# Attention times values with one 64-key by 128-query matmul in place of two 64x64 ones

## The chip, the core and the metric

The kernel runs on one core of one Trainium2 chip. The metric is the device time of one execution in microseconds (us); for several runs, their median. A profiled execution also has a span, from its first to its last instruction, which is a little shorter than its device time. TensorE (PE) does the matmuls and, as instructions of their own (PEld), loads their weights; VectorE (DVE) and ScalarE (ACT) do the elementwise work; GpSimd (POOL) and SyncE (SP) issue most of the DMAs.

## The reference

Sliding-window causal attention, followed by a SwiGLU feed-forward block. There are 8 batches, 8 heads, 576 positions and 64 dimensions per head; the window is 64 keys, the position itself included.

```python
scores = scale * np.matmul(q, k.transpose(0, 1, 3, 2))
mask = (rel >= 0) & (rel < window)        # rel = query position - key position, window = 64
...
attn = attn / (np.sum(attn, axis=-1, keepdims=True) + 1e-09)
out = np.matmul(attn, v)
...
g = x @ w_gate
silu = g * (1.0 / (1.0 + np.exp(-g)))
val = x @ w_val
return (silu * val @ w_out).astype(np.float32)
```

The rows x are the 4608 positions of all batches, each with its 8 x 64 attention outputs; d_model is 512 and d_ff is 1536.

## The kernel before

The 4608 rows are cut into 36 chunks of 128 rows, and for the feed-forward part into 9 groups of 512 rows. A chunk holds two blocks of 64 queries (w = 0 and 1). A batch has 9 blocks, so a block with (2n + w) % 9 == 0 is the first of its batch and has no earlier keys; eight of the 36 chunks hold such a block, here called edge chunks.

Scores (S, matmul on L780). For each head the scores stand with keys on the partitions and queries in the free dimension, in the tile pt. Partitions 0 to 63 hold the chunk's own first 64 keys against all its 128 queries. Partitions 64 to 127 hold, for the queries of block 0, the last 64 keys of the chunk before, and, for those of block 1, the chunk's own last 64 keys. ScalarE takes the exponential into pt (L790), and VectorE multiplies by a mask (L795, function M). The ring pt has 4 buffers, so chunk n uses buffer n % 4.

Probabilities times values. Each head has up to four matmuls, one per half of the partitions (kp = 0 or 1) and query block (w). The weights are a 64x64 piece of pt, and the moving operand is 64 rows of va: the 64 value columns of a head and a column of ones for the sum. The output stands on PSUM partitions 64w to 64w + 63. So each matmul uses a quarter of the array: kp picks the rows, w the columns. For single chunks (n up to 19) this is `A_split`, with the matmul on L832; its two PSUM banks hold heads 0 to 3 and 4 to 7. It runs in two phases (step 0 and 1), so that at one time one bank takes results from rows 0 to 63 only and the other from rows 64 to 127 only: kp = half ^ step. The phases are placed by `A0` and `A1` in the opening, and by `A` afterwards, which puts the scores of the next chunk between them. From chunk 20 on, `A_pair` treats two chunks together (matmul on L905), with three banks: heads 0 to 6 of each chunk, and head 7 of both; here kp = step ^ i for chunk i of the pair, and kp = step for head 7. An edge block leaves out the matmul with the earlier keys.

After that VectorE divides by the sums (L872 to L878, and in pairs from L921 on), the rows are transposed on TensorE (X, L947) or by a DMA on SP's queue (XD, L962), and the feed-forward part follows: gate and value matmuls (FM, L977), tanh on ScalarE (L996), two products on VectorE (L1005, L1007), and the output matmul (OM, L1017).

The order of the work is written out by hand: a list `OPENING` up to about 60 us, and then loops in `build` over groups c, row blocks u and steps s, in which `block(n)` (chunks 12 to 19) and `pair(n)` (20, 22, ..., 34) are put between feed-forward steps. Each engine plays its instructions in the order of recording; a dependency graph from read and write keys adds the semaphore waits. K and Q of chunk n + 4 are transposed by DMA on SP's queue (`TD`, L748 and L751), issued at the end of `block(n)`.

At the place `alone` (L1254), one feed-forward step after `block(19)`, `build` records scores, mask and a merging of the PSUM rings. `block(19)` has already made the scores of chunk 20. The kernel before makes those of chunk 20 there once more, and never those of chunk 21: the pair (20, 21) uses for chunk 21 what chunk 17 left in that buffer of pt.

A second program, `general`, is for inputs out of the usual range; it is built into the kernel, and isn't run here.

Of the kernel before, what the change touches and what calls it, by code (L numbers as in the profile page):

```python
# [14 lines left out]
BPB = S // 64  # L15
# [495 lines left out]
class _Kernel:  # L511
# [292 lines left out]
    def A_split(self, n):  # L804
        g = self.g
        ip = n % self.NP
        va, vp, pt = self.va[n % self.NV], self.va[(n - 1) % self.NV], self.pt[ip]
        bb = [self.bank("a") for _ in range(2)]
        av = [b[:, 0:260].rearrange("p (h x) -> p h x", h=4) for b, _ in bb]
        seq = {}  # L810
        for step in range(2):
            for j in range(4):
                for half in range(2):
                    kp = half ^ step
                    for w in range(2):
                        if kp == w or (2 * n + w) % BPB:
                            seq.setdefault((half, w), []).append((step, j, kp))

        def phase(step):
            def pe(e):  # L820
                for j in range(4):
                    for w in range(2):
                        for half in range(2):
                            q = seq[half, w]
                            key = (step, j, half ^ step)
                            if key not in q:
                                continue
                            kp, h = half ^ step, 4 * half + j
                            vv = vp if kp > w else va
                            ks = slice(64 * kp, 64 * kp + 64)  # L830
                            ws = slice(64 * w, 64 * w + 64)
                            r = e.matmul(av[half][ws, j, :], pt[ks, h, ws], vv[ks, h, 0:65],  # L832
                                         start=key == q[0], stop=key == q[-1])
                return r
            return pe

        vk = [("va", m % self.NV, j) for m in ((n - 1, n) if n else (n,)) for j in range(2)]
        vk += [("va", m % self.NV) for m in ((n - 1, n) if n else (n,))]
        rd = [("pt", ip, 0), ("pt", ip, 1)] + vk
        wr = [bk for _, bk in bb]  # L840

        def run(step, *after):
            return g.op("pe", phase(step), reads=rd, writes=wr, after=list(after))

        return run, bb, av
# [35 lines left out]
    def A_pair(self, n, S0, S1):  # L881


        g = self.g
        nn = (n, n + 1)
        masks = S0()
        banks = [self.bank("a") for _ in range(3)]
        pt = [self.pt[m % self.NP] for m in nn]
        seqs, last = [[], []], {}
        for step in range(2):  # L890
            for h, i in [(h, i) for h in range(7) for i in range(2)] + [(7, 0), (7, 1)]:
                kp = step if h == 7 else step ^ i
                b, col = (2, 65 * i) if h == 7 else (i, 65 * h)
                for w in range(2):
                    if kp == w or (2 * nn[i] + w) % BPB:
                        seqs[step].append((i, h, kp, w, b, col))
                        last.setdefault((b, w), []).append((step, i, h))

        def phase(step):
            def pe(e):  # L900
                for i, h, kp, w, b, col in seqs[step]:
                    ks, ws = slice(64 * kp, 64 * kp + 64), slice(64 * w, 64 * w + 64)
                    vv = self.va[(nn[i] - 1 if kp > w else nn[i]) % self.NV]
                    q, key = last[b, w], (step, i, h)
                    r = e.matmul(banks[b][0][ws, col:col + 65], pt[i][ks, h, ws], vv[ks, h, 0:65],  # L905
                                 start=key == q[0], stop=key == q[-1])
                return r
            return pe

        rd = [("pt", m % self.NP, h) for m in nn for h in range(2)]  # L910
        rd += [("va", m % self.NV, j) for m in (n - 1,) + nn for j in range(2)] + [("va", m % self.NV) for m in (n - 1,) + nn]
        wr = [bk for _, bk in banks]
        first = g.op("pe", phase(0), reads=rd, writes=wr)
        masks = masks + S1()
        g.op("pe", phase(1), reads=rd, writes=wr, after=[first])
        xb = [self.xb[m % 4].rearrange("p (h d) -> p h d", h=H) for m in nn]
        for i, m in enumerate(nn):
            bank, bk = banks[i]
            a = bank[:, 0:455].rearrange("p (h x) -> p h x", h=7)
            rc = self.rc[:, 8 * m:8 * m + 7]  # L920
            g.op("dve", lambda e, rc=rc, a=a: e.reciprocal(rc.unsqueeze(2), a[:, :, 64:65]), reads=[bk],  # L921
                 writes=[("rc", 2 * m), ("rc", 2 * m + 1)])
            rb = rc.unsqueeze(2).to_broadcast([128, 7, 64])
            xo = xb[i][:, 0:7, :]
            g.op("dve", lambda e, xo=xo, rb=rb, a=a: e.tensor_tensor(xo, a[:, :, 0:64], rb, ALU.mult),
                 reads=[bk, ("rc", 2 * m)], writes=[("xb", m % 4, 0), ("xb", m % 4, 1)])
        bank, bk = banks[2]
        a = bank[:, 0:130].rearrange("p (i x) -> p i x", i=2)
        rc = self.rc[:, 8 * n:8 * n + 16].rearrange("p (i h) -> p i h", i=2)[:, :, 7:8]
        g.op("dve", lambda e: e.reciprocal(rc, a[:, :, 64:65]), reads=[bk],  # L930
             writes=[("rc", 2 * m + 1) for m in nn])
        for i, m in enumerate(nn):
            xo = xb[i][:, 7, :]
            r1 = self.rc[:, 8 * m + 7:8 * m + 8]
            g.op("dve", lambda e, xo=xo, r1=r1, i=i: e.tensor_scalar(xo, a[:, i, 0:64], r1, None, ALU.mult),
                 reads=[bk, ("rc", 2 * m + 1)], writes=[("xb", m % 4, 0), ("xb", m % 4, 1)])
        return masks
# [251 lines left out]
    def build(self):  # L1189
# [17 lines left out]
        def block(n):  # L1207
            if n >= NCH:
                return
            load(n + 6)  # L1210
            self.A(n, n + 1 if n + 1 < NCH else None)
            self.XD(n)
            if n + 4 < NCH:
                self.TD(n + 4)

        pair_from = 20

        def pair(n):
            ring, i = self.rot["*"]
            ring = [ring[(i + j) % 8] for j in range(8)]  # L1220
            more = n + 2 < NCH
            for m in (n + 6, n + 7):
                load(m)
            masks = self.A_pair(n, *(lambda m=m: self.S(m, True) if more else [] for m in (n + 2, n + 3)))
            if more:
                self.rot["*"] = ([ring[j] for j in (7, 0, 1, 5, 6, 2, 3, 4)], 0)
            for m in (n + 4, n + 5):
                if m < NCH:
                    self.TD(m)
            for m in (n, n + 1):  # L1230
                self.XD(m)
            for f in masks:
                f()
# [5 lines left out]
        for n in range(pair_from, NCH, 2):  # L1239
            c, r = divmod(n - 6, 4)  # L1240
# [4 lines left out]
        for c in range(2, NFC):  # L1245
            if c == 6:
                self.hint_at = len(self.g.ops)
            for u in range(4):
                late = c == NFC - 1 and u == 3
                for s in range(3):  # L1250
                    self.F(c, 3 * u + s)
                    if s != 1 and (c, u, s) in place:
                        block(place[c, u, s])
                    if (c, u, s) == alone:  # L1254
                        self.S(pair_from)
                        self.M(pair_from)
                        self.share()
                    if s == 1 and not late and c < cp:
                        self.O(c - 1, u, "f" if (c, u, s) in place else "a")
                    if s == 1 and (c, u, s) in place:  # L1260
                        block(place[c, u, s])
                    if c == NFC - 1 and (u, s) in judged:
                        self.judge(judged[u, s])
                if c >= cp and not late:
                    self.O(c - 1, u, "a", "dve" if (c, u) in pairs else "act")
                if (c, u) in pairs:
                    pair(pairs[c, u])
                if late:
                    self.general_at = len(self.g.ops)
                    self.O(c - 1, u)  # L1270
# [46 lines left out]
```

## Time and profile before

| what | value |
|---|---|
| device time, median of 3 runs | 335.17 us (333.53 to 335.91) |
| device time of the profiled execution | 333.98 us |
| span of the profiled execution | 331.4 us |
| matmuls, and as many weight loads | 3511 |
| of these probabilities times values, L832 and L905 | 600 and 488 |
| read from and written to HBM | 37.75 MB and 9.44 MB |

How to read the lines in the prediction. A group line gives the source line, engine, operation and tiles, for matmuls the shape of the weight tile (64*64 means 64 rows by 64 columns), the form of the moving operand, and the count; behind the first bar stand the busy time of the group in us and the mean of one in ns, behind the second the engine's idle time ahead of them. Matmuls are pipelined: their durations overlap, and their ends are modelled by the profiler. A timeline row gives a start, a length from the first start to the last end of a merged run, and the count; two groups that overlap appear as rows that overlap. A row of the table of windows gives the window, its length, and for each engine its busy time and instruction count, then the clock granted to TensorE.

### The profile page before, as it was taken

What the parts mean: (1) busy time and instruction counts of PE and PEld (TensorE: products, weight loads), DVE (VectorE), ACT (ScalarE), POOL (GpSimd) and SP (SyncE); (2) the same over time, 40 slices, a digit from 0 to 9 for tenths busy, and PEclk for the clock granted to TensorE, in tenths of its full rate; (3) what the DMA queues carried; (4) which work ended last, traced back from release to release, by engine and by line L of the source; (5) the groups of instructions that cost most, each with busy time, mean ns of one, the idle gap of its engine ahead of it and who ended that gap; (6) DMA issues with size and microseconds to landing.
All of it is one profiled execution on the core that took longest, in us unless ns stands there. A gap on an engine that the chain in (4) does not pass through costs nothing.

```text
span 331.4 us, 8401 instructions
## 1 busy us (share of the span) xinstructions
PE 323.7 (98%) x3511; PEld 166.2 (50%) x3511; DVE 224.7 (68%) x490; ACT 128.3 (39%) x239; POOL 110.7 (33%) x141
## 2 busy tenths in 40 slices
PE   7799899999999999999999999999999999999996
PEld 3587475555444544445454545454545444444444
DVE  5578896967866866667777777767676776565520
ACT  2756644343333543434242433333424222232222
POOL 7999993194364453333435151000000000000000
PEclk9999999999999999999999999999999999999999
DMA  9999999999999999999999999715140202000012
GB/s 169 150 177 169 171 191 141 171 135 170 169 167 148 191 154 174 173 160 158 149 126 108 135 124 130 128 53 110 47 113 33 65 33 64 34 32 35 35 60 102
DMA packets 169515, 40.19 MB, mean 121 GB/s; under 512 B 155904, under 2 KB 164992, under 8 KB 169472
## 3 DMA queue, kind: packets, MB, share of 16 engines
q0 software_dynamic: 117312, 18.36, 82.8%
q1 hardware_dynamic: 50976, 20.66, 33.3%
q10 hardware_dynamic: 1184, 0.59, 0.7%
q8 instruction: 28, 0.46, 0.6%
q14 instruction: 15, 0.12, 0.1%
HBM read 37.75 MB, written 9.44 MB: 142 GB/s over the span
## 4 chain that ended last, share of the span: by engine, by line
PE 92%; DVE 2%; POOL 2%; DMA 1%; ACT 1%; issue 1%; POOLq 0%
PE ps L977 56%; PE ps L1017 27%; PE ps L780 3%; PE ps L832 2%; PE ps L905 2%; DMA kn<-in_k_dram 1%; PE ps L1049 1%; PE ps L947 1%; DVE uu L1005 1%; POOL va L710 1%; POOL qn L647 1%; DVE hT L1007 0%; PE ps L730 0%; ACT sig L996 0%; ACT qT L664 0%
## 5 line engine op out<-in xcount | busy, mean ns | idle before, releaser
L1005 DVE SCALAR_TENSOR_TENSOR uu<-sig,ps 128x512 bf16<-128x512 bf16 (+2 forms) x122 | 76.0, 623 | 57.5 <-ACT sig L996 57.5
L977 PE MATMUL ps<-xT,Wg 128*128 128x512 bf16 (+2 forms) x488 | 113.7, 355 | 0.3
L977 PE MATMUL ps<-xT,Wv 128*128 128x512 bf16 (+2 forms) x488 | 113.3, 355 | 0.0
L996 ACT ACTIVATE sig<-ps 128x512 bf16<-128x512 f32 (+2 forms) x122 | 66.7, 551 | 82.7 <-PE ps L977 82.4
L1017 PE MATMUL ps<-Wo,hT 128*128 128x512 bf16 x420 | 95.9, 379 | 0.0
L1007 DVE SCALAR_TENSOR_TENSOR hT<-uu,ps 128x512 bf16<-128x512 bf16 (+2 forms) x122 | 76.3, 626 | 4.2
L977 PEld LDWEIGHTS ps<-xT,Wv 128*128 128x128 bf16 x488 | 47.1, 98 | 46.5 <-DVE uu L1005 0.2
L977 PEld LDWEIGHTS ps<-xT,Wg 128*128 128x128 bf16 x488 | 44.6, 98 | 42.2 <-issue 0.4
L1017 PEld LDWEIGHTS ps<-Wo,hT 128*128 128x128 bf16 x420 | 40.9, 98 | 49.2
L647 POOL DMA_DIRECT2D qn<-in_q_dram x38 | 34.9, 932 | 68.2 <-DMA qT<-qn 60.8
L790 ACT ACTIVATE pt<-ps 128x512 bf16<-128x512 f32 x72 | 38.0, 600 | 41.3 <-PE ps L780 41.2
L710 POOL DMA_DIRECT2D va<-in_v_dram x40 | 35.4, 911 | 24.0 <-PE ps L905 19.4
L664 ACT ACTIVATE ost<-ps 128x512 f32<-128x512 f32 (+2 forms) x26 | 15.0, 577 | 64.1 <-PE ps L1017 63.1
L647 POOL DMA_DIRECT2D kn<-in_k_dram x38 | 34.9, 936 | 0.9 <-issue 0.7
L795 DVE TENSOR_TENSOR pt<-pt,mask 128x512 bf16<-128x512 bf16 x64 | 23.8, 419 | 1.2 <-ACT pt L790 1.0
L666 DVE COPY ost<-ps 128x512 f32<-128x512 f32 (+1 forms) x12 | 7.9, 657 | 23.7 <-PE ps L1017 11.9
L878 DVE TENSOR_TENSOR xb<-ps,rc 128x256 bf16<-128x256 f32 x40 | 17.0, 425 | 1.4
L780 PE MATMUL ps<-qT,kT 64*64 64x64 bf16 (+1 forms) x864 | 16.0, 203 | 0.7 <-DVE kT L666 0.3
L780 PEld LDWEIGHTS ps<-qT,kT 64*64 64x64 bf16 x864 | 12.5, 108 | 6.2 <-issue 3.0
L832 PE MATMUL ps<-va,pt 64*64 64x65 bf16 x600 | 12.4, 196 | 1.5 <-issue 1.0
L832 PEld LDWEIGHTS ps<-va,pt 64*64 64x64 bf16 x600 | 8.3, 106 | 8.7 <-issue 3.0
L875 DVE RECIPROCAL rc<-ps 128x4 f32<-128x4 f32 x40 | 7.0, 175 | 6.1 <-PE ps L832 6.1
(57 smaller groups left out, 103.1 us busy)
## 6 DMA issues: line engine op xcount, KB each, us to landing
out_dram<-ost SPq DMA_DIRECT2D x35, 256.0 KB, 3.1
va<-in_v_dram POOLq DMA_DIRECT2D x32, 128.0 KB, 16.8
qn<-in_q_dram POOLq DMA_DIRECT2D x30, 128.0 KB, 15.2
kn<-in_k_dram POOLq DMA_DIRECT2D x30, 128.0 KB, 15.4
Wo<-in_moe_w_out_dram POOLq DMA_DIRECT2D x2, 768.0 KB, 16.2
Wg<-in_moe_w_gate_dram POOLq DMA_DIRECT2D x5, 256.0 KB, 6.7
Wv<-in_moe_w_val_dram POOLq DMA_DIRECT2D x5, 256.0 KB, 7.3
fk<-in_k_dram SPq DMA_DIRECT2D x1, 512.0 KB, 4.9
```

The lines of the kernel that those rows point to most:

```text
L647: self.g.op("pool", lambda e, d=d, a=a: e.dma_start(d, a), writes=ks, dma=True)
L710: g.op("pool", lambda e, d=d, a=a: e.dma_start(d, a), writes=ks, dma=True)
L780: r = e.matmul(sv[h][o:o + 64, c, q0:q1], self.kT[ps, c, kk:kk + 64], qT[ps, c, q0:q1], start=not biased, stop=not biased or c == 3 and kk ...
L790: g.op("act", lambda e, po=po, si=si: e.activation(po, si, ACTF.Exp, scale=SCALE), reads=[bk], writes=[pk])
L795: "dve", lambda e: e.tensor_tensor(po, po, m, ALU.mult), reads=[pk, "mask"], writes=[pk]))
L832: r = e.matmul(av[half][ws, j, :], pt[ks, h, ws], vv[ks, h, 0:65], start=key == q[0], stop=key == q[-1])
L878: g.op("dve", lambda e, xo=xo, rb=rb, a=av[half]: e.tensor_tensor(xo, a[:, :, 0:64], rb, ALU.mult), reads=[bk, ("rc", ir)], writes=[("xb", ...
L977: r = e.matmul(bank[:, 0:n], W[:, kk, f * 128:f * 128 + 128], xT[:, kk, t0:t1], start=(kk == 0), stop=(kk == NK - 1))
L996: self.g.op("act", lambda e: e.activation(sig[:, 0:n], G[:, 0:n], ACTF.Tanh, scale=0.5), reads=[gk], writes=[("sig", i)])
L1005: g.op("dve", lambda e: e.scalar_tensor_tensor(uu[:, 0:n], sig[:, 0:n], 1.0, G[:, 0:n], ALU.add, ALU.mult), reads=[("sig", i), gk], writes ...
L1007: g.op("dve", lambda e: e.scalar_tensor_tensor(hT[:, f, t0:t1], uu[:, 0:n], 0.5, V[:, 0:n], ALU.mult, ALU.mult), reads=[("uu", i), vk], wr ...
L1017: r = e.matmul(OB[:, :], hT[:, f, 128 * u:128 * u + 128], self.Wo[:, f, :], start=(f == 0), stop=(f == NF - 1))
```

## The change

In chunks without an edge block, the two matmuls of a head with kp = 0 become one: its weights are the 64 keys by all 128 queries, and its output is on all 128 PSUM partitions. The two with kp = 1 stay as they are, since their values come from two different chunks or blocks. A full chunk then has 24 matmuls in place of 32. In a pair with an edge chunk the head 7 of both keeps the old form. The order of the matmuls stays what it was, with the merged one at the place of its w = 0 part. At `alone` the scores and mask of chunk 21 are made in place of those of chunk 20.

```diff
@@ A_split
-        seq = {}
+        seq, last, full = [[], []], {}, all((2 * n + w) % BPB for w in range(2))
         for step in range(2):
             for j in range(4):
-                for half in range(2):
-                    kp = half ^ step
-                    for w in range(2):
+                for w in range(2):
+                    for half in range(2):
+                        kp = half ^ step
                         if kp == w or (2 * n + w) % BPB:
-                            seq.setdefault((half, w), []).append((step, j, kp))
+                            if not (full and kp == 0):
+                                seq[step].append((half, j, kp, w, w + 1))
+                            elif w == 0:
+                                seq[step].append((half, j, 0, 0, 2))
+                            last.setdefault((half, w), []).append((step, j))
...
+                for half, j, kp, w0, w1 in seq[step]:
+                    h, q = 4 * half + j, last[half, w0]
+                    vv = vp if kp > w0 else va
+                    ks, ws = slice(64 * kp, 64 * kp + 64), slice(64 * w0, 64 * w1)
+                    r = e.matmul(av[half][ws, j, :], pt[ks, h, ws], vv[ks, h, 0:65],
+                                 start=(step, j) == q[0], stop=(step, j) == q[-1])
@@ A_pair
+        full = [all((2 * m + w) % BPB for w in range(2)) for m in nn]
+        full.append(full[0] and full[1])
...
                     if kp == w or (2 * nn[i] + w) % BPB:
-                        seqs[step].append((i, h, kp, w, b, col))
+                        if not (full[b] and kp == 0):
+                            seqs[step].append((i, h, kp, w, w + 1, b, col))
+                        elif w == 0:
+                            seqs[step].append((i, h, 0, 0, 2, b, col))
                         last.setdefault((b, w), []).append((step, i, h))
...
-                    ks, ws = slice(64 * kp, 64 * kp + 64), slice(64 * w, 64 * w + 64)
+                    ks, ws = slice(64 * kp, 64 * kp + 64), slice(64 * w, 64 * w1)
@@ build
                     if (c, u, s) == alone:
-                        self.S(pair_from)
-                        self.M(pair_from)
+                        self.S(pair_from + 1)
+                        self.M(pair_from + 1)
```

More of the change, by code (lines that the diff above doesn't have):

```diff
@@ L809, in A_split @@
         av = [b[:, 0:260].rearrange("p (h x) -> p h x", h=4) for b, _ in bb]
-        seq = {}
+        seq, last, full = [[], []], {}, all((2 * n + w) % BPB for w in range(2))
         for step in range(2):
             for j in range(4):
-                for half in range(2):
-                    kp = half ^ step
-                    for w in range(2):
+                for w in range(2):
+                    for half in range(2):
+                        kp = half ^ step
                         if kp == w or (2 * n + w) % BPB:
-                            seq.setdefault((half, w), []).append((step, j, kp))
+                            if not (full and kp == 0):
[3 more added lines that the diff above has]
+                            last.setdefault((half, w), []).append((step, j))
         def phase(step):
             def pe(e):
[L821 to L833, printed above, removed]
+                for half, j, kp, w0, w1 in seq[step]:
[4 more added lines that the diff above has]
+                                 start=(step, j) == q[0], stop=(step, j) == q[-1])
                 return r
@@ L900, in pe @@
             def pe(e):
-                for i, h, kp, w, b, col in seqs[step]:
-                    ks, ws = slice(64 * kp, 64 * kp + 64), slice(64 * w, 64 * w + 64)
+                for i, h, kp, w, w1, b, col in seqs[step]:
+                    ks, ws = slice(64 * kp, 64 * kp + 64), slice(64 * w, 64 * w1)
                     vv = self.va[(nn[i] - 1 if kp > w else nn[i]) % self.NV]
```

## The prediction

> **What bounds the kernel now.** I read the page's engine table first, then its slices, then the chain of work that ended last, and then a table of windows that cuts the span into opening, middle and end.
>
> ```profile
> PE 323.7 (98%) x3511; PEld 166.2 (50%) x3511; DVE 224.7 (68%) x490; ACT 128.3 (39%) x239; POOL 110.7 (33%) x141
> ...
> PE 92%; DVE 2%; POOL 2%; DMA 1%; ACT 1%; issue 1%; POOLq 0%
> ```
>
> ```profile
> core 0: us, PE busy (x) PEld busy (x) DVE busy (x) ACT busy (x) POOL busy (x), PEclk, DMA share, GB/s
> 0.00:8.00 8.00, 6.31 (x30) 2.75 (x31) 4.59 (x21) 2.12 (x3) 6.02 (x15) 1.00 1.09 170
> 8.00:13.00 5.00, 4.39 (x150) 2.95 (x148) 2.80 (x9) 4.13 (x8) 5.00 (x8) 1.00 2.17 141
> 13.00:20.00 7.00, 5.40 (x131) 3.63 (x129) 4.10 (x16) 3.64 (x7) 7.00 (x10) 1.00 1.75 165
> 20.00:60.00 40.00, 38.81 (x515) 26.49 (x513) 33.23 (x86) 21.64 (x48) 32.33 (x40) 1.00 1.89 172
> 60.00:150.00 90.00, 90.00 (x1067) 44.46 (x1066) 64.94 (x144) 37.05 (x67) 40.49 (x48) 1.00 1.84 164
> 150.00:271.00 121.00, 120.94 (x1308) 58.30 (x1306) 86.25 (x171) 42.96 (x77) 19.89 (x24) 1.00 0.88 100
> ```
>
> TensorE is the bound: 98% busy, 92% of the chain, and from 60 to 271 us without a gap. Its clock is granted in full. So a microsecond that the changed matmuls add or save in that stretch is a microsecond of the span; no other engine covers it. Before 60 us TensorE is idle for 0.61 + 1.60 + 1.19 = 3.4 us after the start-up; at most that much of an added cost could hide there.
>
> The matmuls that change are two groups, probabilities times values for single chunks (L832) and for pairs (L905):
>
> ```profile
> L832 PE MATMUL ps<-va,pt 64*64 64x65 bf16 x600 | 12.4, 196 | 1.5 <-issue 1.0 <-ACT pt L790 0.2
> L905 PE MATMUL ps<-va,pt 64*64 64x65 bf16 x488 | 7.6, 193 | 0.1
> ...
> L947 PE MATMUL ps<-ident,xb 128*128 128x128 bf16 x40 | 3.6, 220 | 0.4 <-DVE xb L878 0.3
> ```
>
> The means (about 0.19 us) are latencies that overlap; what one costs must be read from the starts. Here is one whole visit, the attention of chunk 19, with the feed-forward matmuls (L977) on either side; each row gives the start, the time from first start to last end, and the count:
>
> ```profile
> 137.10 0.38 PE L977 MATMUL ps<-xT,Wv 128*128 128x512 bf16 x1
> 137.41 0.32 PE L832 MATMUL ps<-va,pt 64*64 64x65 bf16 x16
> 137.56 0.42 PE L780 MATMUL ps<-qT,kT 64*64 64x128 bf16 x24
> 137.81 0.32 PE L832 MATMUL ps<-va,pt 64*64 64x65 bf16 x16
> 138.06 0.39 PE L977 MATMUL ps<-xT,Wg 128*128 128x512 bf16 x1
> ```
>
> Three things are in it. First, the pace: 16 small matmuls take 0.32 us, less the 0.19 of the last one's latency 0.13, so about 0.033 for four. All four 64x64 quarters of the array work at once. Second, from L832 to L780 and back nothing is lost: the next group starts inside the run of the one ahead. Third, something is lost at both ends, where the tile goes from 128x128 to 64x64 and back. For that I need what a 512-column matmul takes in a stream:
>
> ```profile
> 200.46 2.75 PE L1017 MATMUL ps<-Wo,hT 128*128 128x512 bf16 x12
> ```
>
> Eleven steps are 2.75 - 0.38, so 0.216 each (and 65 columns about 0.027). Going in: after the L977 at 137.10 the next could start at 137.32, but L832 starts at 137.41, 0.09 late, and its first four run some 0.02 longer than the rest:
>
> ```profile
> L832 PE MATMUL ps<-va,pt x600: 187/193/215, 10.5 to 137.9; 64*64 64x65 bf16 x150
> ```
>
> That is 0.11. Coming out: the last L832 ends at 138.13 and the first L977 at 138.45, 0.32 apart where a stream has 0.216: 0.10 to 0.11. By starts it is 0.12 from the last small one (138.13 - 0.19) to the L977. The same price shows where only 128 columns follow, so it is not the length of the large matmul:
>
> ```profile
> 8.81 0.45 PE L780 MATMUL ps<-qT,kT 64*64 64x128 bf16 x24
> 9.19 0.40 PE L730 MATMUL ps<-ident,kn 128*128 128x128 bf16 x4
> ```
>
> L780 ends at 9.26; the four L730 end at 9.59, spaced (0.40 - 0.22) / 3 = 0.06, so the first ends at about 9.41, 0.15 to 0.16 later where a stream has 0.06. **A change of the tile's shape costs TensorE about 0.11 us, in either direction; a change of operands, bank or length within one shape costs nothing.** The order of the instructions has 70 such changes before.
>
> **The change part by part.** (1) Merged matmuls. In the 28 chunks that don't hold a batch's first block, the two 64x64 matmuls of a head that share the keys 0 to 63 become one of 64 rows by 128 columns, call it M; the two on rows 64 to 127 stay (q, q). That takes 8 matmuls and 8 weight loads from each such chunk, but 3 fewer in all, because in the pairs (22,23), (26,27) and (30,31) the shared bank of head 7 keeps the old form: 221. TensorE has 3511 matmuls before and 3290 after; M's are 120 + 101.
>
> What the removed instructions are worth: at 0.033 for four, 221 x 0.0082 = 1.8 us if the number of matmuls sets the pace. If the array does, it is nothing: M fills two quarters for the time that two quarters were filled before. Ends: 1.8 us gained, 0 gained. I take 0, since a quarter's 65 columns alone need 0.027 of the 0.033.
>
> What M's weight load may cost: no 64x128 load is in the trace. The nearest is L947's, 128x128 with 128 columns moving, which runs at (0.40 - 0.22) / 3 = 0.06 in the row of the same form above (L730), load included. Were M to run at that pace in place of 0.033: 221 x 0.025 = 5.5 us. Ends 0 and 5.5; I take 0, since a load twice as large is hidden there.
>
> What the order does: the row halves alternate, so M stands between q's nearly everywhere. In a single chunk the first half runs M q q four times (7 changes of shape inside it), the second q M q four times (8), and the entry is a new change only where 64x64 work stands ahead (4 of 15 chunks): 15 x 15 + 4 = 229. A full pair has 30, the last pair 29, a pair with one edge chunk 14: 4 x 30 + 29 + 3 x 14 = 191. Together 420 more, 490 where there were 70.
>
> Does going from 64x64 to 64x128 cost what going from 64x64 to 128x128 does? The trace has no such change. The bounds: 0 (L832 to L780 above, another operand in the same shape) and 0.11 (the shape changes). It is nearer the second: it is a change of tile shape, and that price did not depend on the direction or the length. I take 0.11: 420 x 0.11 = 46.2 us. And once M and its q's are kept apart they no longer run side by side, so each M adds its own 0.027: 221 x 0.027 = 6.0 us.
>
> The Trainium skill, in "TensorEngine Tiling (Array Packing)", section Key Properties, speaks against this change: changing the tiling mode, not just the tile, drains TensorE, and it lists 64x128 as a mode beside 64x64. The trace agrees for 128x128 against 64x64 with 0.11 us; no run here shows 64x64 against 64x128. By that rule the sum is the one below; by the row of L832 to L780 it would be 334.
>
> (2) Chunk 21's scores. The call that made chunk 20's scores a second time now makes chunk 21's. It is the same 24 matmuls, two exponentials and two mask products at the same place, 139.89 us, so it costs nothing by itself. Its inputs are the two transposes that block 17 put on SP's queue:
>
> ```profile
> 139.89 0.45 PE L780 MATMUL ps<-qT,kT 64*64 64x128 bf16 x24
> ```
>
> ```profile
> 124.12 1.32 SPq L748 DMA_TRANSPOSE kT<-kn  x1
> 125.49 2.04 SPq L751 DMA_TRANSPOSE qT<-qn  x1
> ```
>
> They are issued by 127.5, 12 us ahead of their use, and the pair that reads the result begins at 152.7. If that cover went, TensorE would wait there for the rest of a transpose, 1 to 2 us. No DMA moves and no wait is added anywhere; the graph's reads and writes are the same. What is late next is everything behind the slower attention in TensorE's order, by the same amount; VectorE (68%) and ScalarE (39%) have room for it.
>
> **Sum.** The profiled execution took 334.0 us with a span of 331.4. 334.0 + 46.2 + 6.0 = 386.2. That execution lies 1.2 us under the median of the three runs, within their spread.
>
> **The rivals.** A, not slower: hardware that waits only for work in the same rows. M uses rows 0 to 63 and the q's around it rows 64 to 127, so a load for the one half need not wait for the other. For it: M q q on separate halves is just how L832 overlaps now. Against: the 0.11 us is paid although nothing in the data calls for it. Time 334.0, down to 332.2 with the 1.8 us of removed instructions. It decides from a price under 0.008 us per change (420 x 0.008 = 3.4 us, 1%). In the Trainium skill, "TensorE: Matmul & The Clock Gate", section The mechanism of Part 3, says that a weight load overlaps matmuls in flight when its row group differs; no run here shows that across two tile shapes.
>
> B, the wide load sets the pace: as A, but M runs at 0.06: up to 334.0 + 5.5 = 339.5.
>
> C, one direction pays, say where the q's loads can't go ahead but M's can: 216 x 0.11 + 3 = 27, so 361.
>
> D, more than one price: with drains TensorE's work thins out for 2 to 5 us per visit, and the clock could be withdrawn. Before, it is granted in full even at 8 to 13 us where TensorE sits idle for 0.6, which speaks against. The start shows what half a clock costs:
>
> ```profile
> L696 PE MATMUL ps<-wz 128*128 128x512 bf16 x14 | 5.7, 563 | 1.2 <-DVE wz L609 1.2
> ```
>
> 563 against 379 ns. With some 2 us for each of the eight pairs it would be about 402.
>
> E, faster by over 1%: it would need 3.4 us, nearly twice the 1.8 that all removed matmuls are worth; I see no mechanism.
>
> **How the numbers follow.** The forecast 0.56, A 0.22, B 0.07, C 0.08, D 0.03, E 0.04. About 1% is what a measurement of this kernel can tell from no change. The predicted time is the forecast's, 386. Its own range is 372 (0.09 a change, halves still side by side: 334 + 37.8) to 396 (0.12 a change, 6.0 of lost overlap and 5.5 for loads). As A must be inside, the range goes from 333 to 396; it leaves out D, E, and the ends of the others. Faster 0.05 (E and a tail of A), same 0.25 (A and half of B), slower 0.70.
>
> **What would show it.** Right: the group of M's appears as a 64*128 form; a visit like that of 137.32 to 138.06 grows from 0.74 to about 2.6 us (15 x 0.11 + 8 x 0.027 more), the pair at 220 us by 3.7; M and q starts lie 0.13 to 0.14 apart; PEclk stays full. A would show M and q's starting together and visits of 0.74 or less; B visits of about 0.9; C a gap on one side of M only; D a PEclk below 9. I am wrong outright if the shape change between 64x64 and 64x128 starts within a few ns, for all but 6 us of the sum hang on it.

## The result and the profile after

The changed kernel takes 400.26 us in the median of four runs (398.90 to 401.71), the kernel before 335.03 (333.53 to 335.91): 1.195 times as long, with an interval of 1.189 to 1.201. That is 65.2 us more, where 51 were forecast (386), and 4 us above the upper end of the range. Here and below, times are medians of all executions, while the ratios leave out any execution that is more than 1.5% above the fastest of the same kernel.

The profiled execution of the changed kernel took 401.71 us with a span of 399.9. First its page: the engine table, then from the slices TensorE's busy tenths and the clock granted to it, and from the chain its shares by line.

```profile
PE 390.1 (98%) x3250; PEld 207.9 (52%) x3290; DVE 226.7 (57%) x490; ACT 130.0 (32%) x239; POOL 110.9 (28%) x141
...
PE   8999999999999999999999999999999999999997
...
PEclk9869989999889899989899989998999899999999
...
PE ps L979 49%; PE ps L1019 23%; PE ps L829 9%; PE ps L907 7%; PE ps L780 3%; DMA fq<-in_q_dram 2%; ACT pt L790 1%; PE ps L949 1%; PE ps L1051 1%; DVE uu L1007 1%; PE ps L730 0%; PE ps L759 0%; ACT sig L998 0%; ACT qT L664 0%; DVE hT L1009 0%
```

TensorE is still 98% busy and still the chain. Probabilities times values (now L829 and L907) grew from about 3% of the chain to 16%. And the clock, granted in full before, has eights and a six in its row. (3250 of the 3290 matmuls have a record. About half of the missing ones are the first feed-forward matmul behind an attention visit, as at 128.16 below.)

The two groups, by form:

```profile
L829 PE MATMUL ps<-va,pt 64*64 64x65 bf16 x360 | 32.3, 210 | 0.3
L829 PE MATMUL ps<-va,pt 64*128 64x65 bf16 x120 | 24.3, 202 | 0.2 <-ACT pt L790 0.2
L907 PE MATMUL ps<-va,pt 64*64 64x65 bf16 x286 | 22.9, 208 | 0.1
L907 PE MATMUL ps<-va,pt 64*128 64x65 bf16 x101 | 19.4, 200 | 0.0
```

There are 120 + 101 merged matmuls, as counted. The 64x64 ones now have a mean of 208 to 210 ns, not 193 to 196: two thirds of them take some 214 ns now, as in the profile before only those right behind a change of shape did.

One visit of a full chunk, as for the kernel before, in the timeline of TensorE:

```profile
125.11 0.38 PE L979 MATMUL ps<-xT,Wv 128*128 128x512 bf16 x1
125.42 1.19 PE L829 MATMUL ps<-va,pt 64*128 64x65 bf16 x12
126.40 0.46 PE L780 MATMUL ps<-qT,kT 64*64 64x128 bf16 x24
126.67 1.33 PE L829 MATMUL ps<-va,pt 64*64 64x65 bf16 x12
128.16 0.38 PE L979 MATMUL ps<-xT,Wg 128*128 128x512 bf16 x1 [0.16 <-issue]
```

Twelve matmuls take 1.19 us where sixteen took 0.32. From 125.33 (125.11 + 0.216) to the first L979, which has no record and stands 0.216 ahead of the row at 128.16, are 2.61 us, where the visit before took 0.74. The starts inside, from narrow windows of the same timeline (each row begins at a merged matmul or at the first of its two neighbours; length and count go with the window):

```profile
125.42 0.20 PE L829 MATMUL ps<-va,pt 64*128 64x65 bf16 x1
...
125.55 0.35 PE L829 MATMUL ps<-va,pt 64*64 64x65 bf16 x3
...
125.70 0.35 PE L829 MATMUL ps<-va,pt 64*128 64x65 bf16 x3
...
125.83 0.22 PE L829 MATMUL ps<-va,pt 64*64 64x65 bf16 x2
```

From M to its neighbours 0.13 us, from them to the next M 0.15: a head takes 0.28 us, and took 0.033.

Now the clock. The table of windows, for two full pairs and the 3.40 us behind each, and then for a pair with an edge chunk and what follows:

```profile
core 0: us, PE busy (x) PEld busy (x) DVE busy (x) ACT busy (x) POOL busy (x), PEclk, DMA share, GB/s
189.59:194.72 5.13, 4.97 (x97) 3.73 (x98) 0.81 (x2) 2.17 (x4) 0.00 (x0) 1.00 0.64 104
194.75:198.15 3.40, 3.40 (x9) 1.17 (x9) 3.30 (x12) 0.60 (x1) 2.29 (x3) 0.50 0.87 90
230.42:235.55 5.13, 4.97 (x98) 3.73 (x98) 0.81 (x2) 2.17 (x4) 0.00 (x0) 1.00 0.41 105
235.71:239.11 3.40, 3.40 (x9) 1.21 (x8) 3.33 (x11) 0.60 (x1) 3.40 (x4) 0.50 1.00 109
211.82:215.00 3.18, 3.02 (x98) 2.44 (x99) 0.80 (x2) 2.06 (x4) 0.00 (x0) 1.00 0.56 121
215.00:218.41 3.41, 3.41 (x16) 1.57 (x16) 3.31 (x12) 1.19 (x2) 1.37 (x2) 1.00 0.78 67
```

Behind a full pair the granted clock is 0.50, and 9 matmuls stand where 16 do at the full clock. That happens behind all five full pairs (4.9 to 5.1 us each; at the last one the drop begins 1 us ahead of the end) and none of the three with an edge chunk (3.1 to 3.2 us), and behind some of the single chunks. All drops last 3.41 us or a multiple; in this execution they sum to 44 us. The busy column does not show why: TensorE counts as busy for 4.97 of the 5.13 us ahead of the drop.

The drops also begin on one grid: any two of them begin a whole number of 3.413 us apart. That tells which single chunks set one off. In this execution seven of them take 2.58 us, from the first matmul of probabilities times values to the end of the last. The three that lie whole between two points of the grid have a drop behind them (at 109.41, 136.72 and 174.27 us); the four that a point of the grid cuts have none.

### The profile page after: what moved, and what is told of

Its sections match the earlier page's. It is cut to its first block, busy times and chain, and to the rows that moved or that the text cites. A ratio compares the mean times of both kernels' runs of the same rounds, so it can differ in the third digit from the quotient of the medians.

```text
span 399.9 us, 7918 instructions
## 1 busy us (share of the span) xinstructions
PE 390.1 (98%) x3250; PEld 207.9 (52%) x3290; DVE 226.7 (57%) x490; ACT 130.0 (32%) x239; POOL 110.9 (28%) x141
## 4 chain that ended last, share of the span: by engine, by line
PE 94%; ACT 2%; DMA 2%; issue 1%; DVE 1%
PE ps L979 49%; PE ps L1019 23%; PE ps L829 9%; PE ps L907 7%; PE ps L780 3%; DMA fq<-in_q_dram 2%; ACT pt L790 1%; PE ps L949 1%; PE ps L1051 1%; DVE uu L1007 1%; PE ps L730 0%; PE ps L759 0%; ACT sig L998 0%; ACT qT L664 0%; DVE hT L1009 0%
## 5 line engine op out<-in xcount | busy, mean ns | idle before, releaser
L979 PE MATMUL ps<-xT,Wv 128*128 128x512 bf16 (+2 forms) x479 | 121.2, 375 | 0.5
L979 PE MATMUL ps<-xT,Wg 128*128 128x512 bf16 (+2 forms) x464 | 116.2, 374 | 3.5 <-issue 2.7
L998 ACT ACTIVATE sig<-ps 128x512 bf16<-128x512 f32 (+2 forms) x122 | 66.5, 549 | 120.9 <-PE ps L979 120.5
L1019 PE MATMUL ps<-Wo,hT 128*128 128x512 bf16 x415 | 97.5, 385 | 0.4 <-issue 0.2
L979 PEld LDWEIGHTS ps<-xT,Wv 128*128 128x128 bf16 x488 | 49.8, 103 | 52.0 <-issue 8.0
L979 PEld LDWEIGHTS ps<-xT,Wg 128*128 128x128 bf16 x488 | 46.8, 102 | 45.6 <-issue 7.0
L647 POOL DMA_DIRECT2D qn<-in_q_dram x38 | 33.6, 892 | 84.8 <-DMA qT<-qn 81.0
L829 PE MATMUL ps<-va,pt 64*64 64x65 bf16 (+1 forms) x480 | 40.9, 208 | 0.5 <-ACT pt L790 0.2
L829 PEld LDWEIGHTS ps<-va,pt 64*64 64x64 bf16 (+1 forms) x480 | 27.5, 102 | 16.9 <-issue 3.8
L664 ACT ACTIVATE ost<-ps 128x512 f32<-128x512 f32 (+2 forms) x26 | 15.0, 577 | 65.2 <-PE ps L1019 64.2
L647 POOL DMA_DIRECT2D kn<-in_k_dram x38 | 33.5, 892 | 0.6 <-PE ps L730 0.6
L907 PE MATMUL ps<-va,pt 64*64 64x65 bf16 (+1 forms) x387 | 29.9, 206 | 0.1
L907 PEld LDWEIGHTS ps<-va,pt 64*64 64x64 bf16 (+1 forms) x387 | 20.9, 102 | 8.3 <-issue 0.4
L923 DVE RECIPROCAL rc<-ps 128x7 f32<-128x7 f32 x16 | 3.2, 200 | 27.4 <-PE ps L907 27.4
```

The lines of the kernel that those rows point to most:

```text
L647: self.g.op("pool", lambda e, d=d, a=a: e.dma_start(d, a), writes=ks, dma=True)
L664: self.g.op("act", lambda e: e.activation(d, a, ACTF.Copy), reads=rk, writes=wk)
L979: r = e.matmul(bank[:, 0:n], W[:, kk, f * 128:f * 128 + 128], xT[:, kk, t0:t1], start=(kk == 0), stop=(kk == NK - 1))
L998: self.g.op("act", lambda e: e.activation(sig[:, 0:n], G[:, 0:n], ACTF.Tanh, scale=0.5), reads=[gk], writes=[("sig", i)])
L1019: r = e.matmul(OB[:, :], hT[:, f, 128 * u:128 * u + 128], self.Wo[:, f, :], start=(f == 0), stop=(f == NF - 1))
```

## The experiments

The theory: a change of the weight tile's shape drains the array (the next matmul waits until those in flight are nearly through), some 0.11 us each, and where such drains follow each other for longer than about 3.4 us the clock is halved for the next 3.4. The rivals: the merged matmul or its wide load is dear by itself; the second part of the change costs something; the clock falls with the changes of shape as such.

**The second part alone.** The kernel before with this edit:

```diff
-                        self.S(pair_from)
-                        self.M(pair_from)
+                        self.S(pair_from + 1)
+                        self.M(pair_from + 1)
```

> The kernel before with the change's second part alone: scores of chunk 21 in place of the second set for chunk 20; all matmuls 64x64. My theory (the whole loss comes from changes of tile shape and what they do to the clock): no difference, 335 us, within 1 us. Rival (the new scores wait for a transpose or delay the pair behind them): 1 to 2 us more.

335.09 us in 12 runs against 335.00; ratio 0.9989 (0.9970 to 1.0008). It costs nothing. All of the loss is in the first part.

**The same matmuls in another order.** A function `regroup` sorts each phase into runs of so many merged matmuls and twice as many others, merged ones first in the first phase and last in the second. With 99 all of a phase stand together (in `A_pair` likewise):

```diff
+        seq = [regroup(x, lambda y: y[4] - y[3] == 2, i == 0, 99) if i in (0, 1) else x for i, x in enumerate(seq)]
```

> The changed kernel with the same 221 merged matmuls, but within each phase all merged ones stand together (ahead of the 64x64 ones in the first phase, behind them in the second). 126 changes of tile shape in place of 490. My theory (0.11 us per change, 0.027 us per merged matmul that no longer runs beside others, and a clock that falls only where work is thin for long): 335 + 56 x 0.11 + 221 x 0.027 = 347 us, clock full. Rival (the merged matmul or its wide weight load is dear by itself, 65 us / 221 = 0.3 us each, whatever the order): 400 us.

342.92 us; 1.0238 (1.0214 to 1.0262). The same 221 merged matmuls with the same loads cost 7.9 us in this order and 65 in the other. A price of the merged matmul by itself falls. Its groups have the short means back:

```profile
L844 PE MATMUL ps<-va,pt 64*64 64x65 bf16 x360 | 12.4, 196 | 0.2
L844 PE MATMUL ps<-va,pt 64*128 64x65 bf16 x120 | 8.9, 192 | 0.2 <-ACT pt L803 0.2
L924 PE MATMUL ps<-va,pt 64*64 64x65 bf16 x286 | 7.1, 194 | 0.1
L924 PE MATMUL ps<-va,pt 64*128 64x65 bf16 x101 | 5.3, 191 | 0.0
```

The 4 us under the expected 347 lie partly in the opening: by 70 us of the kernel before, this one is 1.45 us behind, where seven full chunks at 2 x 0.11 + 8 x 0.027 make 3.1.

**Half of the changes.** M M q q q q in place of M q q M q q:

```diff
+        seq = [regroup(x, lambda y: y[4] - y[3] == 2, i == 0, 2) if i in (0, 1) else x for i, x in enumerate(seq)]
```

> The changed kernel with the merged matmuls in twos: M M q q q q in place of M q q M q q. The same instructions, 280 changes of tile shape. My theory: 335 + 210 x 0.11 + 221 x 0.027 = 364 us, and up to 5 us more for what is left of the clock drops. Rival (the cost goes with the number of merged matmuls): 400 us.

361.76 us; 1.084 (1.079 to 1.089), with a mean clock of 0.986 to 0.991. With the grouped order that gives (27.3 - 7.9) / (280 - 126) = 0.126 us per change, drops of the clock included.

**One phase grouped, the other as it was.**

```diff
+        seq = [regroup(x, lambda y: y[4] - y[3] == 2, i == 0, 99) if i in (1,) else x for i, x in enumerate(seq)]
```

> The changed kernel with the merged matmuls grouped in the second phase alone; the first phase keeps M q q. 310 changes of shape. A full pair's visit falls from 5.1 to about 3.2 us, a single chunk's from 2.7 to about 1.7. My theory: 335 + 240 x 0.11 + 221 x 0.027 = 367 us with no or few clock drops (up to 5 us more). Rival (the clock falls in proportion to the changes): its share of the loss, some 13 us at 420 more changes, would be 7 to 8 us: 375 us, with a mean clock of about 0.97.

364.23 us; 1.089 (1.083 to 1.095). That is (29.8 - 7.9) / (310 - 126) = 0.119 us per change. Its clock shows one drop:

```profile
PEclk9999999999999999999999999999999998999999
```

**Merged matmuls in single chunks alone.**

```diff
@@ A_pair
-        full = [all((2 * m + w) % BPB for w in range(2)) for m in nn]
+        full = [False for m in nn]
```

> Merged matmuls in single chunks alone, pairs as before: 120 of them, 299 changes of shape. My theory: 335 + 229 x 0.11 + 120 x 0.027 = 363 us, and for the clock drops of the first 180 us (seven in the changed kernel, one twice as long) up to 8 x 1.7 = 13 us: 363 to 376. If the parts add up, this loss and that of the pairs alone (the rest of 65 us) make the whole. Rival (a price per merged matmul): 335 + 120 x 0.295 = 370 us; it can't be told from mine here, but the row-merged kernel beside it can be compared with it.

370.18 us; 1.106 (1.102 to 1.111). This and the kernel ahead have about as many changes of shape, 299 and 310, but this one is 6 us slower, with about half as many merged matmuls. The difference is in the clock, 0.963 to 0.971 on the mean where the other has 0.995 in all but one of its runs:

```profile
PEclk9969998999699999998999999999999999999999
```

Here two chunks on end, in the opening and after it, make drained stretches of 4.6 to 5.8 us, in part at the halved clock; there no visit of any kind is longer than 3.9. So the number of changes does not set the clock.

**Pairs alone.**

```diff
@@ A_split
-        seq, last, full = [[], []], {}, all((2 * n + w) % BPB for w in range(2))
+        seq, last, full = [[], []], {}, False
```

> Merged matmuls in pairs alone (101 of them), single chunks as before: 261 changes of tile shape. My theory: 335 + 191 x 0.11 + 101 x 0.027 = 359 us, and 1.7 us for each drop of the clock, which I expect behind each of the five full pairs and behind none of the three with an edge chunk: 367. If the losses add up, it is the whole loss less that of the singles alone: 65 - 36 = 29, so 364. Rival (a price per merged matmul, 65 / 221): 335 + 101 x 0.295 = 365, but then with the clock full.

366.43 us; 1.091 (1.083 to 1.098), mean clock 0.962 to 0.976, which a price per merged matmul would have left full. In its profile drops begin in or behind four of the five full pairs and none of the edge pairs. (The full pair without one, from 237.41 to 242.00 us, has a point of the grid of 3.413 us near its middle, at 239.48, where the dense scores also stand.) Singles and pairs add up: 35.7 + 30.8 = 66.5 against 65.2.

**All matmuls of a full chunk 64x128** (in `A_pair` likewise).

```diff
-                            if not (full and kp == 0):
+                            if not full:
...
-                                seq[step].append((half, j, 0, 0, 2))
+                                seq[step].append((half, j, kp, 0, 2))
```

> All matmuls of probabilities times values in full chunks are 64x128, those on rows 64 to 127 too, with the earlier chunk's values for both query blocks (so the values of the second block's own last keys are left out: the output is not the reference's). 16 matmuls per full chunk, 183 changes of shape, and the row halves can work side by side again. My theory: 335 + 113 x 0.11 = 347 us if a wide weight load is hidden as a narrow one is, and 353 if a pair of wide ones takes 0.06 in place of 0.033 us. Rival (wide loads are dear by themselves): 400 us or more, since there are some 440 of them.

351.87 us in the median of four runs; 1.040 (1.034 to 1.047) from the two of them at 346.05 and 351.22. The four differ by their clock: 346.05 with the clock full on the mean, and 351.2 to 353.4 with 0.976 to 0.979. The first is at the expected 347. In the profile, of the run of 353.40 us, the drops begin in the three pairs with an edge chunk, where 64x64 and 64x128 alternate in this kernel and a visit takes 4.5 to 4.8 us. A visit of a single chunk:

```profile
120.39 0.29 PE L829 MATMUL ps<-va,pt 64*128 64x65 bf16 x8
120.62 0.45 PE L780 MATMUL ps<-qT,kT 64*64 64x128 bf16 x24
121.00 0.29 PE L829 MATMUL ps<-va,pt 64*128 64x65 bf16 x8
```

Eight wide ones on alternating row halves take 0.29 us, less the 0.19 of a latency 0.10, so 0.03 for two: the pace of four quarters before. The load of 128 columns costs nothing extra. And L780 no longer overlaps them: 64x64 work behind 64x128 work waits.

**A merging by rows.** In full single chunks the second query block takes both row halves in one matmul of 128 rows by 64 columns:

```diff
@@ A_split
+        if full:
+            seq = [[x for j in range(4) for x in ((step, j, 2, 1, 2), (1 - step, j, 0, 0, 1))]
+                   + [(step, j, 1, 0, 1) for j in range(4)] for step in range(2)]
...
+                    ks, ws = slice(0, 128) if kp == 2 else slice(64 * kp, 64 * kp + 64), slice(64 * w0, 64 * w1)
...
@@ A_pair
-        full = [all((2 * m + w) % BPB for w in range(2)) for m in nn]
+        full = [False for m in nn]
```

> In full single chunks another merging with as many matmuls (24): for the second query block both row halves in one matmul of 128 rows by 64 columns, for the first block two of 64x64 as before; pairs as before. 298 changes of shape, between 64x64 and 128x64. Does a change of the rows alone cost what a change of the columns does? If any change of shape drains the array: 335 + 228 x 0.11 + 120 x 0.048 (less side by side) = 366 us, and up to 13 us for the clock. Rival (only the columns' mode drains): 335 + 6 = 341 us.

372.42 us; 1.115 (1.107 to 1.122). A change of the rows alone costs as much: from 128x64 to 64x64 and back the starts are 0.14 to 0.15 us apart, and the groups have the long means again.

```profile
L840 PE MATMUL ps<-va,pt 64*64 64x65 bf16 x360 | 33.1, 208 | 0.0
L840 PE MATMUL ps<-va,pt 128*64 128x65 bf16 x120 | 26.9, 224 | 0.5 <-ACT pt L790 0.2
```

The weight tile here has 64 columns, like its neighbours; so the price isn't that of a load of another width either.

**Dense work put into the full pairs.** First one burst between the two phases:

```diff
+        def burst(e):
+            for _ in range(8):
+                r = e.matmul(b0[:, 0:455], wz[:, 0:128], wz[:, 0:455], start=False, stop=False)
+            return r
...
+        if full[2]:
+            first = g.op("pe", burst, reads=["wz"], writes=[banks[0][1]], after=[first])
```

> The changed kernel with eight 128x128 matmuls of zeros (455 columns, accumulated onto the first bank, so the result stays) between the two phases of each of the five full pairs. They cost 5 x (8 x 0.19 + 0.11) = 8.2 us. My theory of the clock (it falls to half for 3.41 us after a window of 3.41 us with too little work, which all five full pairs of 5.1 us hold): with the burst no window is thin throughout, the five drops behind the pairs go, 5 x 1.7 = 8.5 us come back, and the time stays at 400 us, with the mean clock up from 0.944 to about 0.965. Rival (the clock falls because of the changes of shape themselves): the drops stay, 408 us.

403.85 us; 1.203 (1.200 to 1.206), between the two expectations. The mean clock of four of its five runs is 0.962 to 0.966, where the changed kernel's is 0.944 to 0.948, as the theory has it; but the time that it gave back is only about half of what the burst costs. The fifth run, the one with a profile, took 414.03 us with a mean clock of 0.934: in it a drop begins behind the first half of three of the five full pairs, and one behind a pair with an edge chunk. Each half of a pair is still 2.2 us of drains, and single chunks of 2.6 us sometimes set off a drop; one burst was too little to settle it. So three bursts, none of the drained stretches of a full pair then being longer than some 1.5 us with the scores in them:

```diff
+                    if k == 12 and full[2]:
+                        zeros(e, 260 if step == 0 else 455)
...
+        if full[2]:
+            first = g.op("pe", lambda e: zeros(e, 455), reads=["wz"], writes=[banks[0][1]], after=[first])
```

> The changed kernel with three bursts of 128x128 matmuls of zeros (accumulated onto the first bank, so the result stays) in each of the five full pairs: in the middle of the first phase (8 of 260 columns), between the phases and in the middle of the second (5 of 455 each). No thin stretch of a full pair is then longer than about 1.3 us. They cost 5 x (8 x 0.11 + 10 x 0.19 + 3 x 0.11) = 15.5 us at the full clock; there are 505 changes of shape. My theory (the clock falls after 3.41 us of thin work): the five drops behind the full pairs go and give back 5 x 1.7 = 8.5 us: 400.3 + 15.5 - 8.5 = 407 us, mean clock about 0.97. Rival (the clock falls with the changes of shape themselves): 416 us, mean clock no higher than 0.95.

409.98 us; 1.220 (1.212 to 1.228), nearer to the theory's 407 than to the rival's 416. The profiled execution, the fastest of the four, took 405.43, with a mean clock of 0.975. In it none of the five full pairs is followed by a drop; what is left are 13.65 us at half the clock in the opening and two drops behind single chunks. Two of the full pairs, with what follows:

```profile
227.66:236.05 8.39, 8.17 (x116) 5.24 (x117) 0.81 (x2) 2.17 (x4) 0.00 (x0) 1.00 0.58 96
236.05:239.46 3.41, 3.41 (x16) 1.57 (x16) 3.31 (x12) 1.19 (x2) 3.27 (x4) 1.00 0.67 43
312.35:320.74 8.39, 8.17 (x116) 5.24 (x117) 0.81 (x2) 2.17 (x4) 0.00 (x0) 1.00 0.10 33
320.74:324.15 3.41, 3.41 (x16) 1.56 (x16) 3.31 (x12) 1.19 (x2) 0.00 (x0) 1.00 0.08 16
```

16 matmuls again where there were 9, with 505 changes of shape, more than in the changed kernel. With the pair of kernels of 299 and 310 changes this speaks against changes of shape as such, and for thin work, as the cause of the drops. The other three executions have mean clocks of 0.954 to 0.966, and where their drops lie no trace shows.

How thin the work must be can be estimated from the twelve profiles of all these kernels. Cut each at its grid of 3.413 us, and count the work in a window in matmuls of 512 columns on the full array, of which 16 fill it (a 64x64 tile with 65 columns counts 65/512 of a quarter, and a matmul without a record is put in where its load stands). Leave out the first 8 us, the end, and the windows that are themselves at half the clock. Of the windows with less than 4 of 16, all 23 are followed by a drop; of those with 4 to 7, 23 of 61; of those with more, none of 1084. Changes of shape do not sort them: two windows with 2 changes each are followed by a drop, and windows with 16 of them not always. What decides between 4 and 7 stays open. The theory above was too simple in this: it is not the length of a stretch that counts but how little work is left in one window of the grid, and a visit of 2.6 us can be enough.

## Why the prediction was wrong, point by point

*The bound.* Right. TensorE is 98% busy in both kernels, and nothing hid the added time but a little of the opening.

*The price of a change of shape.* Right in size, and the open question was answered as forecast: 64x64 against 64x128 costs what 64x64 against 128x128 does. 0.11 us was forecast per change; M and its neighbours start 0.13 and 0.15 us apart, of which about 0.03 is their own stream. The Trainium skill's rule in "TensorEngine Tiling (Array Packing)", Key Properties, that a change of mode drains the array, agrees with these runs, for a change of the rows or of the columns alone too, at about 0.11 us each.

*The visits.* 2.6 us was forecast for a single chunk, and 2.61 measured. A full pair was to take 3.7 us more: 1.34 + 3.7 = 5.0, and it takes 5.13 less the 0.22 of the unrecorded matmul, 4.9.

*The wide load* at nothing: right (0.03 us for two). *The removed instructions* at nothing: right as far as it shows; the grouped order has all of them removed and is 7.9 us slower. *Chunk 21's scores* at nothing: right (0.9989).

*The sum.* It was short, because rival D came on top of the forecast and not in its place. The step that failed is the one that set the clock aside: "Before, it is granted in full even at 8 to 13 us where TensorE sits idle for 0.6, which speaks against." An idle time of 0.6 us in 5 says nothing on 5 us without a dense stretch, and the trace of before holds no stretch of that kind. (The next row of the same table, 13 to 20 us, has 1.6 us of idle time in 7; in another profile of nearly the same kernel, shown in the last section, that part of the opening did set off a drop.) So the clock's loss, put at nothing, was some 16 us. That D's total, 402, is close is partly luck: it takes some 2 us for each of the eight pairs, while each drop costs about half of 3.41, 1.7 us, behind five pairs, four places among the single chunks behind 80 us, and in the opening. (Its 563 against 379 ns are durations of matmuls that overlap; what a drop costs shows in the count, 9 matmuls in place of 16.) D had a chance of 0.03, and the range ended below it.

How the 65.2 us divide: the one-phase kernel, with the clock nearly full, has 29.8 us for 240 changes more; less one drop of 1.7 that is 0.117 each, and 420 of them make 49. (From the grouped kernel to this one it is 20.2 us for 184 changes, 0.110 each, and 7.9 + 364 x 0.110 makes 48.) So some 48 to 49 us are drains and work that no longer runs side by side (52.2 forecast), and some 16 are the clock. From the other side, the drops of the profiled execution that lie behind 80 us sum to 31 us, of which half is 15.4; what the 14 us of drops in the opening cost can't be told from there, since work there also waits for other things.

*Rivals A, B, C* fall: no change was free, no pace of the loads showed, and both directions pay.

## What to carry to other kernels

Count the changes of the weight tile's shape in TensorE's order, not the matmuls: merging two 64x64 matmuls into one 64x128 removes an instruction that was free and adds two drains where its neighbours stay 64x64. If shapes must be mixed, group them: the same instructions took 343 us grouped and 400 alternating. And where a change thins TensorE's work for some 2.5 us on end or more, put the loss at the halved clock that can follow into the sum; the busy column won't show it, the row of the granted clock will. No version here beats the kernel before; with chunk 21's scores it takes the same 335 us.

## What the runs showed of the hardware beyond that

The clock falls to exactly 0.50 for 3.41 us or a multiple, though TensorE counts as busy for 97% of the stretch ahead of it. The Trainium skill, in "TensorE: Matmul & The Clock Gate", Part 1, has the two states and the window of 3.4 us, and ties the low state to an idle window; here TensorE was not idle, and drained work, with matmuls 0.13 to 0.15 us apart, was enough.

Even the kernel with only the scores changed has one such drop in its profiled execution (and, by a mean clock of 0.995, in five others of the twelve), behind a stretch of the opening with TensorE busy for 1.35 of 3.42 us, by the table of windows:

```profile
14.24:17.66 3.42, 1.35 (x70) 0.80 (x58) 0.79 (x4) 1.48 (x3) 3.42 (x6) 1.00 1.45 164
17.66:21.07 3.41, 3.15 (x44) 3.02 (x43) 1.81 (x7) 1.31 (x4) 3.41 (x6) 0.50 2.02 169
```

Executions of the kernel before, too, have a mean clock of 1.000 in some runs and 0.995 in others (one window of 3.41 us at half in 333 is 0.005), so the profile that was read for the prediction did not hold all that this clock does.

The Trainium skill, in "TensorE: Matmul & The Clock Gate", section The mechanism of Part 3, has a weight load overlap matmuls in flight when its row group differs. Across two tile shapes little of that is left: the load of M's neighbours, on rows 64 to 127, starts 0.13 us behind M's (125.55 against 125.42 us), when M has 0.07 of its 0.20 to go by its record; in the kernel before, 16 loads of one shape start within 0.11 us (the visit at 137.41).
